# Loading k and q in pairs of blocks and transposing them in 64-column halves, in a fused attention and MLP kernel

## The chip, the core and the metric

The kernel runs on one core of one Trainium2 chip. The metric is device time in microseconds (us), the median of several runs. A core has TensorE (PE, with its weight loads shown as PEld), VectorE (DVE), ScalarE (ACT), GpSimd (POOL), SyncE (SP) and 16 DMA engines.

## What is computed

Sliding-window attention with a linear distance bias, then a two-layer MLP with a squared ReLU. Batch 8, 8 heads, 576 tokens, head size 64; the MLP goes from 512 to 2048 and back, over 4608 tokens.

```
scores = scale * q @ k.T ; bias = -slope[h] * |i - j|
mask   = (i - j >= 0) & (i - j < 128)
attn   = softmax(where(mask, scores + bias, -1e9))
x      = (attn @ v), heads side by side, as 4608 x 512
out    = square(relu(x @ w_in)) @ w_out
```

All inputs are float32 in device memory; the kernel works in bfloat16 and gives float32.

## The kernel before

Each batch entry is cut into five blocks of tokens: four of 128 and one of 64, 40 blocks in all. For each block m the function `attention` does these steps:

- q and k, loaded with tokens on partitions (a tile `kq`, 128 partitions, k in the first half of a row, q in the second), are turned so that the head dimension lies on partitions (`kqT`). For blocks 0 to 9 (`m < KQ_DMA`) TensorE does it: eight transposes of 128x128 into one PSUM bank (`tp`), evicted in two copies, one for k, one for q. For later blocks a DMA transpose from SyncE does it.
- One burst of score matmuls (`ps_s`, L361) with this block's and the previous block's keys. Each uses 64 rows of the array, and neighbouring ones use the two halves.
- ScalarE takes the exponential (L374), VectorE multiplies with a mask that holds bias and window (L382), TensorE multiplies with v (`pv`, L397; a column of ones in `vt` gives the sum of the row), VectorE normalises into `x` (L418, L423).
- x is transposed too (`xp`, L442, into `xT`), by TensorE for the first 13 blocks.

The MLP works on groups of 512 tokens. `fc_step` makes 128 hidden units for a group (`h`, L477), or, for the first two groups, several of them for a part of the group as its tokens become ready: group 0 in parts of 128 tokens, with four sets of hidden units for each step, so that one step needs one quarter of w_in. ScalarE applies the ReLU (L487) and VectorE or ScalarE squares (L495, L497). The second layer is plain for group 0 (`o`, L628), and for the other groups a scheme with seven products instead of eight (`o`, L559), with sums on VectorE (L523).

All loads are DMAs issued from GpSimd, which also convert to bfloat16 (k, q and v at L290, w_in at L256, w_out at L263). A load of a block has one piece of 64 floats for each token and head. `FIRST` (L162) is the order of the loads for the first ten blocks: `b3` means k, q and v of block 3, `i1` a quarter of w_in, `o1` a quarter of w_out.

The order of instructions on every engine is fixed before the launch. Each piece of work is a task with possible engines and estimated durations, a key (lower first), what it depends on and the buffers that it takes and frees. `Plan.order` runs through estimated time and picks, for each engine, the task that can start first, and among equals the one with the lowest key. The instructions are then emitted in that order; on the chip each engine works through its own list in order and waits where data are late.

Buffers are rings: a new user of a tag takes the slot of the oldest user, once all that read it are done. PSUM has "h" (2 banks: first-layer results, and for the first batch entry also `tp` and `xp`), "o" (2 banks: second-layer results, `pv` of the first five blocks, every second first-layer step of group 0) and "a" (4 banks: a burst of scores takes all four; `tp` and `xp` of later batch entries take one). In SBUF, `kq` has 4 slots, `vt` 6 and `kqT` 4.

Of the kernel before, what the change touches and what calls it, by code (L numbers as in the profile page):

```python
# [9 lines left out]
BF16 = mybir.dt.bfloat16  # L10
# [132 lines left out]
def kernel(  # L143
    ctx: ExitStack, tc: tile.TileContext, q, k, v, moe_w_in, moe_w_out, out
):
    nc = tc.nc

    B, H, S, D = q.shape
# [6 lines left out]
    NKB = (S + 127) // 128  # L155
    blk = [min(128, S - kb * 128) for kb in range(NKB)]
    C = d_model // 128
# [1 line left out]
    NG = NT // 512  # L159
    NBLK = B * NKB  # L160

    FIRST = "b0 i0 b1 i1 b2 i2 b3 i3 b4 b5 b6 o0 b7 o1 b8 o2 b9 o3"  # L162
    SPLIT = ([(0, 128), (128, 256), (256, 384), (384, 512)], [(0, 256), (256, 512)])

    KQ_DMA, X_DMA = 10, 13
# [3 lines left out]
    psum = ctx.enter_context(tc.tile_pool(name="psum", bufs=2, space=bass.MemoryType.PSUM))  # L169
    work = ctx.enter_context(tc.tile_pool(name="work", bufs=2))  # L170

    ident = const.tile([128, 128], BF16)
# [8 lines left out]
    def ring(name, n, shape):  # L181
        return [const.tile(shape, BF16, name=f"{name}_{i}") for i in range(n)]
# [4 lines left out]
    kq = ring("kq", size["kq"], [128, 2, d_model])  # L187
    vt = ring("vt", size["v"], [128, H, D + 1])
    kqT = ring("kqT", size["kqT"], [128, 2 * C, 128])
# [3 lines left out]
    plan = Plan({"h": 2, "o": 2, "a": 4, "rec": 4, "rt": 3, "g": 2, "S": 2, "osb": 4,  # L193
                 "s1": 2, "u2": 2, "x1": 2, **size})

    def act(n):
        return n * 0.84 + 90.0

    def dve(n, rate=1):
        return n / rate / 0.96 + 72.0  # L200

    def mm(n):
        return max(n, 64) / 2.4 + 1.5
# [12 lines left out]
    t_ident = plan.add({"DVE": 230.0}, -9e5 - 1, build_ident, [t_iota])  # L216
# [11 lines left out]
    def place(h):  # L228
        c, half = divmod(h, 2)
        return 4 * (c // 2) + 2 * half + c % 2  # L230
# [12 lines left out]
    t_ones = plan.add({"DVE": 1200.0}, -9e5 + 1, ones)  # L243


    def load(key, ns, emit, deps=(), acq=()):
        return plan.add({"POOL": 900.0}, key, emit, deps, acq, dma=ns)
# [29 lines left out]
    s_in, t_in = {}, {}  # L277

    def load_block(m, key):
# [4 lines left out]
        for i, (nm, src) in enumerate((("k", k), ("q", q), ("v", v))):  # L284
# [5 lines left out]
                nc.gpsimd.dma_start(o, src[b, :, kb * 128:kb * 128 + n, :].rearrange("h s d -> s h d"))  # L290
            t_in[m, nm] = load(key + 0.01 * i, 1050.0 * n / 128, emit, [t_ones] if nm == "v" else [], [sl])

    for i, what in enumerate(FIRST.split()):
        {"b": load_block, "i": load_w_in, "o": load_w_out}[what[0]](int(what[1:]), -9e5 + i)
    for m in range(2 * NKB, NBLK):
        load_block(m, -5e5 + m)

# [2 lines left out]
    chain = {"tp": [], "s": [], "pv": [], "xp": []}  # L300

    def copy(task, o, i):
        if task.eng == "DVE":
            nc.vector.tensor_copy(o, i)  # L304
        else:
            nc.scalar.activation(o, i, AF.Copy)  # L306

    def attention(m):
        b, kb = divmod(m, NKB)
        n = blk[kb]  # L310
        due = (b * S + kb * 128 + n) / 4 - 192 - 40
        first = b == 0
# [4 lines left out]
        sk = sk_of[m] = Slot("kqT")  # L317
        both = {"ACT": act(C * n), "DVE": dve(C * n, 2)}
        if kq_by_dma:
            def turn_kq():  # L320
                nc.sync.dma_start_transpose(kqT[sk.idx], kq[s_in[m, "k"].idx].rearrange("s t f -> s (t f)"))
            t_kq = [plan.add({"SP": 2000.0}, due - 80, turn_kq, [t_in[m, "k"], t_in[m, "q"]], [sk],
                             [s_in[m, "k"]], dma=1400.0)]
        else:
            slot = Slot("h" if first else "a")
            last = None
            for i in range(2 * C):
                def emit(i=i):
                    if i == 0:
                        slot.tile = psum.tile([128, 1024], BF16, tag=slot.tag, bufs=plan.bufs[slot.tag], name="tp")  # L330
                    nc.tensor.transpose(slot.tile[:, i * 128:(i + 1) * 128],  # L331
                                        kq[s_in[m, "k"].idx][:, i // C, (i % C) * 128:(i % C + 1) * 128], ident)
                last = plan.add({"PE": mm(128)}, due - 56, emit,
                                [last, t_ident, t_in[m, "kq"[i // C]]] + ([t_in[m, "q"]] + chain["tp"] if i == 0 else []),
                                [slot, sk] if i == 0 else [], [s_in[m, "k"]] if i == 2 * C - 1 else [])
            chain["tp"] = [last]
            t_kq = []
            for i in range(2):
                def evac(i=i):
                    copy(t_kq[i], kqT[sk.idx][:, i * C:(i + 1) * C, 0:n],  # L340
                         slot.tile[:, i * 512:(i + 1) * 512].rearrange("p (c s) -> p c s", c=C)[:, :, 0:n])
                t_kq.append(plan.add(both if first else {("DVE", "ACT")[i]: both[("DVE", "ACT")[i]]},
                                     due - 56, evac, [last], [], [slot]))
        t_kq_of[m] = t_kq


# [41 lines left out]
        for hf in range(2):  # L388
            slot_v = Slot("o" if m < 5 else "h")
            last = None  # L390
            for hi in range(4):
                h = 4 * hf + hi
                for part, mk in parts:
                    def emit(h=h, hi=hi, part=part, mk=mk, slot_v=slot_v):
                        if hi == 0 and part == p0:
                            slot_v.tile = psum.tile([128, 512], FP32, tag=slot_v.tag, bufs=plan.bufs[slot_v.tag], name="pv")
                        nc.tensor.matmul(  # L397
                            slot_v.tile[:, hi * (D + 1):(hi + 1) * (D + 1)],
                            Pt[sP.idx][:, place(h), part, :], vt[s_in[mk, "v"].idx][:, h, :],
                            start=part == p0, stop=part == 1)  # L400
                    rel = []
                    if hf == 1 and hi == 3:
                        if part == 0 or kb == NKB - 1:
                            rel.append(s_in[mk, "v"])
                        if part == 1:
                            rel.append(sP)
                    new = hi == 0 and part == p0
                    last = plan.add({"PE": mm(D + 1)}, due - 12 + 4 * hf, emit,
                                    [last, t_P[place(h) // 2], t_in[mk, "v"]]
                                    + (t_P[2 * hf:2 * hf + 2] + chain["pv"] if new else []),  # L410
                                    ([slot_v] + ([sx] if hf == 0 else [])) if new else [], rel)
# [18 lines left out]
        t0 = b * S + kb * 128  # L430
        if x_by_dma:
            def turn_x():
                nc.sync.dma_start_transpose(xT[:, :, t0:t0 + n], xt[sx.idx][0:n, :])
            t_xT[b, kb] = plan.add({"SP": 1280.0}, due, turn_x, t_norm, [], [sx], dma=1800.0)
        else:
            slot_x = Slot("h" if first else "a")
            last = None
            for c in range(C):
                def emit(c=c):
                    if c == 0:  # L440
                        slot_x.tile = psum.tile([128, 1024], BF16, tag=slot_x.tag, bufs=plan.bufs[slot_x.tag], name="xp")
                    nc.tensor.transpose(slot_x.tile[:, c * 128:(c + 1) * 128],  # L442
                                        xt[sx.idx][:, c * 128:(c + 1) * 128], ident)
                last = plan.add({"PE": mm(128)}, due, emit, [last] + t_norm,
                                [slot_x] if c == 0 else [], [sx] if c == C - 1 else [])

            def evac():
                copy(t_xT[b, kb], xT[:, :, t0:t0 + n],
                     slot_x.tile[:, 0:512].rearrange("p (c t) -> p c t", c=C)[:, :, 0:n])
            t_xT[b, kb] = plan.add(both if first else {"DVE": both["DVE"]}, due, evac, [last], [], [slot_x])  # L450

    sk_of, t_kq_of = {}, {}
    for m in range(NBLK):
        attention(m)

# [187 lines left out]
    key = 0  # L643
# [5 lines left out]
    for g in range(NG):  # L649
# [8 lines left out]
        key = base + (64 if g == 0 else 128)  # L658
# [36 lines left out]
```

## Time and profile before

| | |
|---|---|
| median of 3 runs | 307.44 us (307.18 to 307.74) |
| the profiled execution | 308.27 us |
| its span in the profile | 306.1 us |
| busy: PE, DVE, ACT, POOL | 289.8, 212.2, 200.0, 107.6 us |
| granted TensorE clock | 1.0 |
| moved by DMA | 39.31 MB, 128 GB/s on average |

The span is the time between the first and the last record of the program, about 2.2 us less than the execution's own time. In the rows of the profile, "L331" is line 331 of the kernel, `out<-in` names tiles of the program, "x80" counts instructions, and the time in brackets is how long the engine stood idle before the row and what released it. The ends of matmuls are modelled: one with 128 columns is shown with 0.22 us though the next one can start after 0.06, so start times are what is to be compared.

### The profile page before, as it was taken

To read this page: it belongs to the slowest core of one execution; us is meant where nothing else is said; L and a number is where in the kernel's file an instruction comes from. 1 tells how busy PE (TensorE), PEld (TensorE's weight loads), DVE (VectorE), ACT (ScalarE), POOL (GpSimd) and SP (SyncE) were. 2 spreads that over 40 slices of the span, in tenths; PEclk is the share of its full clock that TensorE was granted. 3 is DMA by queue.
4 is the path that set the end of the run, shared out by engine and by line. 5 is a ranking of instruction groups with operands and counts; after the bars stand their busy time and mean duration, and the time that the engine had idled before them with its cause. 6 is when DMAs were issued, how large, how long until landed. Compare 5 with 4: busy or idle time off the path is not lost.

```text
span 306.1 us, 7855 instructions
## 1 busy us (share of the span) xinstructions
PE 289.8 (95%) x3076; PEld 205.9 (67%) x3076; DVE 212.2 (69%) x633; ACT 200.0 (65%) x395; POOL 107.6 (35%) x133
## 2 busy tenths in 40 slices
PE   1489999999999999999999999999999999999995
PEld 1279987686866677666666666666766676666783
DVE  4348888749968786678758776677677785545622
ACT  4178894759769666767767787777667785564410
POOL 8747938626265444226361327132200000000000
PEclk9999999999999999999999999999999999999999
DMA  8999999999999999999999999999884112201223
GB/s 60 179 175 166 151 189 173 130 184 139 151 151 144 164 157 169 155 154 182 165 153 166 156 139 149 130 165 146 139 55 120 30 42 62 69 0 36 69 72 103
DMA packets 170901, 39.31 MB, mean 128 GB/s; under 512 B 158064, under 2 KB 170352, under 8 KB 170864
## 3 DMA queue, kind: packets, MB, share of 16 engines
q0 software_dynamic: 116736, 18.36, 93.9%
q1 hardware_dynamic: 54128, 20.46, 41.3%
q8 instruction: 24, 0.39, 0.5%
q14 instruction: 13, 0.11, 0.1%
HBM read 36.70 MB, written 9.44 MB: 151 GB/s over the span
## 4 chain that ended last, share of the span: by engine, by line
PE 92%; DMA 3%; DVE 2%; POOL 2%; ACT 1%; issue 0%; POOLq 0%; DVEq 0%
PE h L477 42%; PE o L559 32%; PE ps_s L361 6%; PE pv L397 6%; PE o L628 4%; DMA kq<-in_q_dram 3%; PE tp L331 1%; POOL kq L290 1%; PE xp L442 1%; ACT kqT L306 1%; DVE w_mix L273 0%; DVE kqT L304 0%; POOL vt L290 0%; DVE osb L593 0%; POOL w_in_sb L256 0%
## 5 line engine op out<-in xcount | busy, mean ns | idle before, releaser
L477 PE MATMUL h<-xT,w_in_sb 128*128 128x512 bf16 (+2 forms) x832 | 150.8, 316 | 0.3 <-DVE x L423 0.3
L487 ACT ACTIVATE rt<-h 128x512 bf16<-128x512 f32 x144 | 86.0, 600 | 61.9 <-PE h L477 54.2
L477 PEld LDWEIGHTS <-w_in_sb 128*128 128x128 bf16 x832 | 71.0, 99 | 35.4 <-DVE x L423 0.8
L374 ACT ACTIVATE P<-ps_s 128x512 bf16<-128x512 f32 (+1 forms) x160 | 71.1, 520 | 9.7 <-PE ps_s L361 9.5
L495 DVE TENSOR_TENSOR g<-rt 128x512 bf16<-128x512 bf16 x91 | 38.3, 422 | 35.1 <-ACT rt L487 34.4
L382 DVE TENSOR_TENSOR P<-P,masks 128x512 bf16<-128x512 bf16 (+1 forms) x160 | 54.4, 364 | 8.0 <-ACT P L374 6.5
L559 PEld LDWEIGHTS <-g 128*128 128x128 bf16 x512 | 47.9, 98 | 15.1
L290 POOL DMA_DIRECT2D kq<-in_k_dram x40 | 34.2, 855 | 55.6 <-DMA kqT<-kq 48.4
L290 POOL DMA_DIRECT2D vt<-in_v_dram x40 | 34.1, 856 | 52.8 <-PE pv L397 46.6
L559 PEld LDWEIGHTS <-S 128*128 128x128 bf16 x384 | 35.8, 98 | 11.7 <-issue 0.7
L559 PE MATMUL o<-w_mix,S 128*128 128x256 bf16 x256 | 38.7, 273 | 0.0
L559 PE MATMUL o<-w_mix,g 128*128 128x256 bf16 x256 | 37.5, 273 | 0.0
L559 PE MATMUL o<-w_out_sb,g 128*128 128x256 bf16 x256 | 36.9, 273 | 0.0
L290 POOL DMA_DIRECT2D kq<-in_q_dram x40 | 34.3, 857 | 2.0 <-DMA kq<-in_k_dram 1.3
L497 ACT ACTIVATE g<-rt 128x512 bf16<-128x512 bf16 x53 | 33.5, 632 | 1.3
L423 DVE TENSOR_TENSOR x<-pv,rec 128x256 bf16<-128x256 f32 (+1 forms) x80 | 33.3, 417 | 1.1
L397 PEld LDWEIGHTS <-P 128*128 128x128 bf16 x576 | 27.3, 98 | 8.9 <-DVE P L382 1.2
L397 PE MATMUL pv<-vt,P 128*128 128x65 bf16 x576 | 31.5, 194 | 0.6 <-DVE P L382 0.6
L418 DVE RECIPROCAL rec<-pv 128x4 f32<-128x4 f32 (+1 forms) x80 | 14.2, 177 | 14.6 <-PE pv L397 14.2
L361 PEld LDWEIGHTS <-kqT 64*128 64x128 bf16 x576 | 15.7, 96 | 11.1 <-issue 8.9
L361 PE MATMUL ps_s<-kqT 64*128 64x128 bf16 (+1 forms) x320 | 20.1, 216 | 0.8 <-DVE kqT L304 0.8
L361 PE MATMUL ps_s<-kqT,kqT 64*128 64x128 bf16 (+1 forms) x256 | 17.0, 214 | 1.4 <-ACT kqT L306 1.4
(41 smaller groups left out, 190.6 us busy)
## 6 DMA issues: line engine op xcount, KB each, us to landing
out_dram<-osb SPq DMA_DIRECT2D x35, 256.0 KB, 4.3
kq<-in_k_dram POOLq DMA_DIRECT2D x32, 128.0 KB, 7.1
kq<-in_q_dram POOLq DMA_DIRECT2D x32, 128.0 KB, 7.4
vt<-in_v_dram POOLq DMA_DIRECT2D x32, 128.0 KB, 8.2
w_in_sb<-in_moe_w_in_dram POOLq DMA_DIRECT2D x4, 512.0 KB, 9.8
w_out_sb<-in_moe_w_out_dram POOLq DMA_DIRECT2D x4, 512.0 KB, 10.0
kq<-in_k_dram POOLq DMA_DIRECT2D x8, 64.0 KB, 9.2
kq<-in_q_dram POOLq DMA_DIRECT2D x8, 64.0 KB, 8.9
```

Of the source, the lines that this page charges most:

```text
L290: nc.gpsimd.dma_start(o, src[b, :, kb * 128:kb * 128 + n, :].rearrange("h s d -> s h d"))
L361: nc.tensor.matmul(slot_s[2 * (c // 2) + half].tile.rearrange("p (c t q) -> p c t q", c=2, t=2)[:, c % 2, part, 0:n], kqT[sk_of[mk].idx][r ...
L374: nc.scalar.activation(view(Pt[sP.idx][:, 2 * i:2 * i + 2]), view(slot_s[i].tile.rearrange("p (c t q) -> p c t q", c=2, t=2)), AF.Exp, bia ...
L382: nc.vector.tensor_tensor(pt, pt, view(masks[:, 2 * i:2 * i + 2]), op=ALU.mult)
L397: nc.tensor.matmul(slot_v.tile[:, hi * (D + 1):(hi + 1) * (D + 1)], Pt[sP.idx][:, place(h), part, :], vt[s_in[mk, "v"].idx][:, h, :], star ...
L418: nc.vector.reciprocal(srec.tile[0:n, :], pv[0:n, :, D])
L423: nc.vector.tensor_tensor(xt[sx.idx][0:n, hf * 256:(hf + 1) * 256].rearrange("p (h e) -> p h e", h=4), pv[0:n, :, 0:D], srec.tile[0:n, :]. ...
L477: nc.tensor.matmul(slot.tile[:, f * w:(f + 1) * w], w_in_sb[:, cc, (fc + f) * 128:(fc + f + 1) * 128], xT[:, cc, g * 512 + lo:g * 512 + hi ...
L487: nc.scalar.activation(srt.tile, slot.tile, AF.Relu, bias=0.0, scale=1.0)
L495: nc.vector.tensor_tensor(o, i, i, op=ALU.mult)
L497: nc.scalar.activation(o, i, AF.Square)
L559: nc.tensor.matmul(bank.tile[:, t * 256:(t + 1) * 256], left(g, what, j)[:, t * 128:(t + 1) * 128], right(by, j), start=opens and j == 0 a ...
```

## The change

For blocks 0 to 9, k and q are no longer loaded block by block, but for a pair of neighbouring blocks: 256 tokens (64 for the fifth block of a batch entry, which stands alone). A tile `kq` holds one of k or q, and each partition has two neighbouring tokens: row p holds, for each head, the 64 values of token 2p and then the 64 of token 2p+1. A piece of a load is thus 128 floats. v is loaded block by block as before, and `FIRST` gets a new order, in which `s0` is k and q of the first pair and `v0` is v of block 0.

TensorE transposes such a tile in halves of 64 columns: one instruction takes one head of one of the two tokens of a partition (64 columns), and writes 64 partitions of PSUM and 128 columns. Even heads go to the lower 64 partitions, odd heads to the upper. k and q have a bank each. For a pair of blocks there are 16 halves for k and 16 for q.

The evictions are still two for each block, one for k and one for q. They read the bank with the two tokens of a pair 128 elements apart, so that `kqT` is written in the order of the tokens. For the second batch entry k is evicted by ScalarE and q by VectorE (before: k by VectorE, q by ScalarE).

```diff
-    FIRST = "b0 i0 b1 i1 b2 i2 b3 i3 b4 b5 b6 o0 b7 o1 b8 o2 b9 o3"
+    FIRST = "s0 i0 v0 v1 i1 s1 v2 i2 v3 i3 s2 v4 s3 v5 v6 o0 s4 v7 o1 v8 o2 s5 v9 o3"
...
+    def load_pair(i, key):
+        b, pr = divmod(i, (NKB + 1) // 2)
+        ms = [m for m in (b * NKB + 2 * pr, b * NKB + 2 * pr + 1) if m < (b + 1) * NKB]
+        n = sum(blk[m - b * NKB] for m in ms)
+        t0 = pr * 256
+        for j, (nm, src) in enumerate((("k", k), ("q", q))):
+            sl = Slot("kq")
+
+            def emit(src=src, sl=sl):
+                nc.gpsimd.dma_start(
+                    kq[sl.idx][0:n // 2].rearrange("p t f -> p (t f)").rearrange("p (h e) -> p h e", h=H),
+                    src[b, :, t0:t0 + n, :].rearrange("h (p u) d -> p h (u d)", u=2))
+            t = load(key + 0.01 * j, 1150.0 * n / 256, emit, [], [sl])
+            for m in ms:
+                s_in[m, nm], t_in[m, nm] = sl, t
...
-            slot = Slot("h" if first else "a")
-            last = None
-            for i in range(2 * C):
...
-                    nc.tensor.transpose(slot.tile[:, i * 128:(i + 1) * 128],
-                                        kq[s_in[m, "k"].idx][:, i // C, (i % C) * 128:(i % C + 1) * 128], ident)
-                last = plan.add({"PE": mm(128)}, due - 56, emit,
...
+            for j, nm in enumerate("kq"):
+                if kb % 2 == 0:
+                    turned[nm] = slot = Slot("h" if first else "a"), []
+                    last = None
+                    for i, g in [(i, g) for i in range(2 * C) for g in range(2)]:
...
+                            nc.tensor.transpose(
+                                slot.tile[g * 64:(g + 1) * 64, i * 128:(i + 1) * 128],
+                                kq[s_in[m, nm].idx].rearrange("p t f -> p (t f)").rearrange(
+                                    "p (c g u d) -> p c u g d", c=C, g=2, u=2)[:, i // 2, i % 2, g], ident)
+                        last = plan.add({"PE": mm(128) / 2}, due - 56, emit,
...
+                slot, (done_tp,) = turned[nm]
+
+                def evac(j=j, slot=slot):
+                    o = kqT[sk.idx][:, j * C:(j + 1) * C, 0:n].rearrange("p c (s u) -> p c s u", u=2)
+                    s0 = 64 * (kb % 2)
+                    copy(t_kq[j], o, slot.tile.rearrange("p (c u s) -> p c s u", c=C, u=2)[:, :, s0:s0 + n // 2])
+                t_kq.append(plan.add(both if first else {("ACT", "DVE")[j]: both[("ACT", "DVE")[j]]},
+                                     due - 56, evac, [done_tp], [sk] if j == 0 else [], [slot]))
```

More of the change, by code (lines that the diff above doesn't have):

```diff
@@ L291, in load_block, with load_v, emit @@
             t_in[m, nm] = load(key + 0.01 * i, 1050.0 * n / 128, emit, [t_ones] if nm == "v" else [], [sl])
+    def load_v(m, key):
+        b, kb = divmod(m, NKB)
+        n = blk[kb]
+        sl = s_in[m, "v"] = Slot("v")
+        def emit():
+            nc.gpsimd.dma_start(vt[sl.idx][0:n, :, 0:D], v[b, :, kb * 128:kb * 128 + n, :].rearrange("h s d -> s h d"))
+        t_in[m, "v"] = load(key, 1050.0 * n / 128, emit, [t_ones], [sl])
+    def load_pair(i, key):
[12 more added lines that the diff above has]
+                s_in[m, nm], t_in[m, nm] = sl, t
     for i, what in enumerate(FIRST.split()):
-        {"b": load_block, "i": load_w_in, "o": load_w_out}[what[0]](int(what[1:]), -9e5 + i)
+        {"s": load_pair, "v": load_v, "i": load_w_in, "o": load_w_out}[what[0]](int(what[1:]), -9e5 + i)
     for m in range(2 * NKB, NBLK):
@@ L324, in attention @@
         else:
-            slot = Slot("h" if first else "a")
-            last = None
-            for i in range(2 * C):
[L328 to L331, printed above, removed]
-                                        kq[s_in[m, "k"].idx][:, i // C, (i % C) * 128:(i % C + 1) * 128], ident)
-                last = plan.add({"PE": mm(128)}, due - 56, emit,
-                                [last, t_ident, t_in[m, "kq"[i // C]]] + ([t_in[m, "q"]] + chain["tp"] if i == 0 else []),
-                                [slot, sk] if i == 0 else [], [s_in[m, "k"]] if i == 2 * C - 1 else [])
@@ L336, in attention @@
-            chain["tp"] = [last]
-            t_kq = []
[L338 to L343, printed above, removed]
+            t_kq = []
@@ new lines, in attention, with emit @@
+            for j, nm in enumerate("kq"):
[3 more added lines that the diff above has]
+                    for i, g in [(i, g) for i in range(2 * C) for g in range(2)]:
+                        def emit(i=i, g=g, nm=nm, slot=slot[0]):
+                            if i == 0 and g == 0:
+                                slot.tile = psum.tile([128, 1024], BF16, tag=slot.tag, bufs=plan.bufs[slot.tag], name="tp")
+                            nc.tensor.transpose(
[3 more added lines that the diff above has]
+                        last = plan.add({"PE": mm(128) / 2}, due - 56, emit,
+                                        [last, t_ident, t_in[m, nm]] + (chain["tp"] if i == 0 else []),
+                                        [slot[0]] if i == 0 and g == 0 else [],
+                                        [s_in[m, nm]] if i == 2 * C - 1 and g == 1 else [])
+                    chain["tp"] = [last]
+                    slot[1].append(last)
+                slot, (done_tp,) = turned[nm]
[5 more added lines that the diff above has]
+                                     due - 56, evac, [done_tp], [sk] if j == 0 else [], [slot]))
@@ L450, in attention @@
             t_xT[b, kb] = plan.add(both if first else {"DVE": both["DVE"]}, due, evac, [last], [], [slot_x])
-    sk_of, t_kq_of = {}, {}
+    sk_of, t_kq_of, turned = {}, {}, {}
     for m in range(NBLK):
```

## The prediction

> **What bounds the kernel now.** I read four views of the profile, in this order: busy shares and slices on the page, the waits of TensorE from 17 us on, the timeline of the first 30 us, the transfers of those microseconds.
>
> ```profile
> PE 289.8 (95%) x3076; PEld 205.9 (67%) x3076; DVE 212.2 (69%) x633; ACT 200.0 (65%) x395; POOL 107.6 (35%) x133
> PE   1489999999999999999999999999999999999995
> DMA  8999999999999999999999999999884112201223
> ```
>
> ```profile
> PE ps_s L361 <- ACT kqT L306: 0.7, 1, 0.7
> PE o L559 <- DVE osb L593: 0.5, 1, 0.5
> PE h L477 <- DVE x L423: 0.3, 1, 0.3
> ```
>
> TensorE is busy in every slice but the first three and the last. The second fence is all that it waits for after 17 us: 1.5 us in 289. So the end is set by two things only: when dense work starts, and how much of it there is. The DMA engines are full in the first 30 of 40 slices, but after 17 us no TensorE wait names a load; transfers that finish earlier there are worth nothing by themselves.
>
> The start looks like this (start, length, engine, line, operation):
>
> ```profile
> 5.09 0.60 PE L331 MATMUL tp<-ident,kq 128*128 128x128 bf16 x4 [5.09 <-DMA kq<-in_k_dram]
> 6.35 0.61 PE L331 MATMUL tp<-ident,kq 128*128 128x128 bf16 x4 [0.65 <-DMA kq<-in_q_dram]
> 8.97 1.18 PE L397 MATMUL pv<-vt,P 128*128 128x65 bf16 x8 [0.56 <-DVE P L382]
> 10.42 0.42 DVE L423 TENSOR_TENSOR x<-pv,rec 128x256 bf16<-128x256 f32 x1
> 13.38 0.61 PE L331 MATMUL tp<-ident,kq 128*128 128x128 bf16 x4 [3.23 <-DMA kq<-in_k_dram]
> 14.21 0.61 PE L331 MATMUL tp<-ident,kq 128*128 128x128 bf16 x4 [0.22 <-DMA kq<-in_q_dram]
> 14.62 0.63 PE L442 MATMUL xp<-ident,x 128*128 128x128 bf16 x4
> 15.29 0.42 DVE L304 COPY xT<-xp 128x512 bf16<-128x512 bf16 x1
> 16.93 3.24 PE L477 MATMUL h<-xT,w_in_sb 128*128 128x128 bf16 x32
> ```
>
> Block 0 is normalised at 10.84, but its transpose (14.62) stands behind block 1's k and q in TensorE's order, and those land only at 13.4 and 14.2. The first layer starts at 16.93.
>
> **The earlier start: a gain.** The change loads k and q of blocks 0 and 1 first, then the first quarter of w_in, then v of block 0. I need three paces of the DMA engines. The next rows are the issues of q, v and w_in, each one's time to landing (in the same order), and packets in 4 to 6 us, 18 to 20 us and 26 to 28 us.
>
> ```profile
> 2.26 0.89 POOL L290 DMA_DIRECT2D kq<-in_q_dram  x1
> 3.53 1.02 POOL L290 DMA_DIRECT2D vt<-in_v_dram  x1
> 4.55 0.76 POOL L256 DMA_DIRECT2D w_in_sb<-in_moe_w_in_dram  x1
> kq<-in_q_dram POOLq DMA_DIRECT2D x1, 128.0 KB, 4.0
> vt<-in_v_dram POOLq DMA_DIRECT2D x1, 128.0 KB, 4.7
> w_in_sb<-in_moe_w_in_dram POOLq DMA_DIRECT2D x1, 512.0 KB, 7.9
> DMA packets 1437, 0.18 MB, mean 90 GB/s; under 512 B 1437, under 2 KB 1437, under 8 KB 1437
> DMA packets 576, 0.41 MB, mean 203 GB/s; under 512 B 204, under 2 KB 576, under 8 KB 576
> DMA packets 2348, 0.31 MB, mean 156 GB/s; under 512 B 2328, under 2 KB 2348, under 8 KB 2348
> ```
>
> A 128-token load is 1024 packets of 128 bytes. With the engines full (last row, 2328 in 2 us) it takes 0.88 us, or 2 x 16 / 2328 = 13.7 ns of an engine per packet. In 18 to 20 us, 204 such packets use 2.8 of 32 engine-us, so 372 packets of 1 KB take 29.2 / 372 = 78 ns each, and a w_in quarter of 512 of them 2.5 us. A pair load is 1024 packets of 256 bytes, a size that the trace does not have. On a straight line between the two it is 22.9 ns, so 1.47 us for what two loads do in 1.76; at worst it costs twice a small packet (1.76), at best its bytes at 1 KB price, 19.5 ns (1.25). At the very start the packets come slower (1437 in 2 us, 1024 in 1.43 us), GpSimd writing one load per 0.9 to 1.0 us. There a pair load takes about as long as a single one does now: the pair of k and q lands near 5.2 and 6.4 instead of 5.1 and 6.3.
>
> Then comes w_in. In the rows it landed at 12.45 (4.55 + 7.9), 4.2 us after v (8.23). I take those 4.2 again: 10.6. v of block 0 adds 0.88: 11.5. From v to the first layer it needs 1.87 for the products with v and their normalising (8.97 to 10.84), and about 1.2 for the transpose of x and its eviction (0.63 + 0.42 and hand-overs): 3.1, so the first layer starts at 14.6 instead of 16.93. I enter **-2.2**. Bounds: 1.4 if a packet of 256 bytes costs two small ones (0.3 for each of the two pair loads) and the lag lasts a little longer; 3.0 if w_in lands in 3.4 us instead of 4.2 (by its pace alone it takes 2.5). I go no further, because TensorE must still find work at every moment after that start, with pair 1 landing two pair loads after the second w_in quarter.
>
> **More TensorE work: a loss.** In steady state, the transposes and the tiled score matmuls run like this:
>
> ```profile
> 34.04 0.41 PE L397 MATMUL pv<-vt,P 128*128 128x65 bf16 x8
> 34.28 0.39 PE L477 MATMUL h<-xT,w_in_sb 128*128 128x128 bf16 x4
> 36.69 0.61 PE L331 MATMUL tp<-ident,kq 128*128 128x128 bf16 x8
> 37.13 1.22 PE L477 MATMUL h<-xT,w_in_sb 128*128 128x128 bf16 x19
> 38.42 0.29 PE L397 MATMUL pv<-vt,P 128*128 128x65 bf16 x4
> 38.64 0.23 PE L361 MATMUL ps_s<-kqT,kqT 64*128 64x128 bf16 x2
> 39.04 0.22 PE L361 MATMUL ps_s<-kqT 64*128 64x128 bf16 x2
> 39.19 0.30 PE L397 MATMUL pv<-vt,P 128*128 128x65 bf16 x4
> ```
>
> Eight transposes go from 36.69 to 37.13: 55 ns each. Sixteen score matmuls, which use 64 rows of the array each, run two at a time: 14 of them from 38.64 to 39.04, 28.6 ns each. But they start 0.10 us after the four products ahead of them are issued (4 x 30 ns from 38.42, by 8 in 0.24 at 34.04), and the next product comes at 39.19, 0.09 after they end at 39.10. A change of the array's tiling and back costs 0.19 us.
>
> The change has 16 half transposes per tensor and pair: 192 for six pairs, in place of 80. Pair 0's fall into waiting time at the start, so 160 stand against 64 of blocks 2 to 9 (64 x 55 ns = 3.5 us). No row shows a half over 64 columns. Its price lies between 28 ns (two at a time, as the score matmuls) and 56 (one after the other, each still streams 128 columns of the identity). I take 28, since the halves alternate between column groups as the scores do between row groups: 4.5 us, **+0.9**. By 56 it is 9.0, +5.4.
>
> Against 28 speaks the Trainium skill, "TensorEngine Tiling (Array Packing)", Restrictions: column tiling switches the fast weight load off. Its page "TensorE: Matmul & The Clock Gate", LDWEIGHTS, gives columns / 1.2 ns, an estimate of 53 ns for 64 columns. In this trace 128 columns load in 30 ns or less (the eight products at 34.04); no row has a load of 64 columns. If loads of the two column groups can't overlap, the sum goes to its upper end; rival A has that.
>
> Each run of halves also switches the tiling, as today's full transposes do not. k and q of a pair land about 1.4 us apart, so pairs 1, 3 and 4 have two runs each, the two 64-token pairs one: 8 runs x 0.19 = **+1.5** (5 to 10 runs: 1.0 to 1.9).
>
> **Evictions and slots.**
>
> ```profile
> L304 DVE COPY kqT<-tp 128x512 bf16<-128x512 bf16 x9 | 3.7, 422 | 8.0 <-PE tp L331 5.7 <-PE pv L397 1.8 <-ACT kqT L306 0.4
> L306 ACT ACTIVATE kqT<-tp 128x512 bf16<-128x512 bf16 x7 | 4.2, 597 | 8.2 <-DVE kqT L304 7.9 <-PE tp L331 0.2
> L607 DVE TENSOR_TENSOR u<-o,s 128x512 f32<-128x512 f32 x1 | 0.7, 692 | 0.2 <-PE o L559 0.2
> ...
> 45.00:50.00 5.00, 5.00 (x45) 3.14 (x44) 5.00 (x18) 2.39 (x5) 3.41 (x4) 1.00 1.85 180
> ```
>
> There are 20 evictions as before. They now read PSUM with neighbouring elements 128 apart. ScalarE should stay at 597; VectorE lies between 422 and the 692 of an operation that takes one element at a time, so up to 0.27 more, some 3 us over ten copies. The Trainium skill, "VectorE: DVE Perf Modes", asks for steps of one in its doubled mode, which speaks for 692; the copies with steps of one take 422 here, and no row has another step. TensorE's queue of other work hides this, but VectorE is full in 45 to 50 us (5.00 of 5.00), and TensorE once waited on it (0.3): **+0.2** (0 to 0.8). k and q now lie in two banks, so both engines can evict at once; the 0.7 us wait of ps_s behind ACT kqT may go. On the other side, a pair holds both "h" slots until four evictions are done, and two of four "a" slots later, while first-layer steps and the transpose of x want "h". One eviction time of 0.6 to 0.7 for two waiting steps is 1.3; it falls in the densest stretch for pair 1 alone. Together **+0.3** (-0.7 to +1.3). Fewer GpSimd issues (12 for 20) end nothing that is late.
>
> **Sum:** -2.2 + 0.9 + 1.5 + 0.2 + 0.3 = +0.7. The profiled execution took 308.27 (span 306.1 and 2.2 around it), 0.83 over the median of 307.44. The difference of 0.7 in the span is added to the median: **308.1**.
>
> **Rivals.** A: the halves do not run two at a time, or are not tiled by columns at all. +5.4 for +0.9 gives +5.2, 312.6; without tiling the 1.5 of switches go too, 311.1. Nothing in the trace shows column groups side by side; the row groups speak against it. It decides from about 36 ns a half, where it alone adds 1.3.
> B, faster: the loads win more. w_in lands 3.4 us after q, the start is 3.0 earlier, k and q of a pair are transposed in one run (5 runs, 1.0), and the ps_s wait of 0.7 goes without a new one: -3.0 + 0.9 + 1.0 - 0.7 + 0.2 = -1.6, 305.8. For it: the 4.2 us of the first w_in quarter is long against 2.5. Against: TensorE's order is fixed, so any load that is late stops it. It decides where the start gains over 2.9.
> C: packets of 256 bytes cost no less per byte than small ones, and TensorE, in order, waits for pair 1: the gain falls to 0.8, the sum to +2.1, 309.5.
>
> **The numbers.** The forecast has 0.48, A 0.21, B 0.23, C 0.08. A change under 0.2% (0.6 us) can't be told from none, the runs lying from 307.18 to 307.74. The forecast's own range is 306.8 to 309.4; of its 0.48, 0.05 is faster, 0.20 the same and 0.23 slower. So faster 0.28, same 0.20, slower 0.52. The range reaches from 305.9, near B, to 312.6, A.
>
> **What would show it.** The first h matmul near 14.6; pair loads of about 1.5 us; 192 tp matmuls, 32 within about 0.9 us and 0.1 us gaps on both sides; VectorE's kqT copies at 692; TensorE's waits after 17 us still under 3 us. I am wrong if h starts after 16, if 16 halves take 0.9 us, or if new waits on kqT or on loads stand in the dense part.

## The result, and the profile after

The changed kernel took 310.56 us (median of four runs) against 307.31 us: the ratio is 1.0094, with a 95% interval of 1.0068 to 1.0121. One of the four, the profiled one, ran at a granted clock of 0.573 and took 506.76 us; the ratio leaves it out (the median of the other three is 310.41). Run again, as e1 below, the changed kernel took 310.28 us against 308.34 us, 1.0072 (1.0050 to 1.0094). By these two ratios it is slower by 2.2 to 2.9 us where +0.7 was forecast; both medians lie in the stated range of 305.9 to 312.6, but above the likeliest case's own range, which ended at 309.4. The profile shown here is that of e1: span 308.6 us, 2.5 more than before.

The page, busy time by engine, then TensorE's slices and its granted clock:

```profile
PE 293.8 (95%) x3188; PEld 207.5 (67%) x3188; DVE 215.0 (70%) x627; ACT 202.7 (66%) x401; POOL 100.1 (32%) x125
...
PE   2589999999999999999999999999999999999995
...
PEclk9999999999999999999999999999999999999999
```

TensorE is again the engine that is never idle after the start, and it has 112 matmuls more. All its waits that the view names, start included:

```profile
PE tp L359 <- DMA kq<-in_k_dram: 7.1, 2, 5.8
PE pv L430 <- DMA vt<-in_v_dram: 2.0, 1, 2.0
PE ps_s L394 <- DVE kqT L329: 0.8, 1, 0.8
PE xp L475 <- DVE x L456: 0.7, 2, 0.5
PE o L592 <- DVE osb L626: 0.5, 1, 0.5
PE tp L359 <- DMA kq<-in_q_dram: 0.3, 1, 0.3
```

TensorE's timeline of the start (start, length, what; the wait in brackets):

```profile
5.83 1.06 PE L359 MATMUL tp<-ident,kq 128*64 128x128 bf16 x16 [5.83 <-DMA kq<-in_k_dram]
7.19 1.06 PE L359 MATMUL tp<-ident,kq 128*64 128x128 bf16 x16 [0.30 <-DMA kq<-in_q_dram]
...
11.62 0.38 PE L430 MATMUL pv<-vt,P 128*128 128x65 bf16 x4 [1.97 <-DMA vt<-in_v_dram]
...
14.03 0.40 PE L475 MATMUL xp<-ident,x 128*128 128x128 bf16 x2 [0.52 <-DVE x L456]
14.36 0.69 PE L430 MATMUL pv<-vt,P 128*128 128x65 bf16 x5
16.29 1.07 PE L359 MATMUL tp<-ident,kq 128*64 128x128 bf16 x16 [1.24 <-DMA kq<-in_k_dram]
17.29 0.35 PE L430 MATMUL pv<-vt,P 128*128 128x65 bf16 x3
17.44 0.30 PE L510 MATMUL h<-xT,w_in_sb 128*128 128x128 bf16 x1
17.53 0.65 PE L430 MATMUL pv<-vt,P 128*128 128x65 bf16 x8
17.99 1.57 PE L510 MATMUL h<-xT,w_in_sb 128*128 128x128 bf16 x13
19.50 1.06 PE L359 MATMUL tp<-ident,kq 128*64 128x128 bf16 x16
20.49 1.82 PE L510 MATMUL h<-xT,w_in_sb 128*128 128x128 bf16 x18
```

v of block 0 lands at 11.6, as forecast, and x of block 0 is transposed by 14.4. But TensorE's fixed order then wants the transposes of pair 1, whose k lands only at 16.3, and the first layer starts at 17.4, half a microsecond later than before (16.93). By then TensorE has, however, done eight of block 1's products with v and the transposes of pair 1's k, which the kernel before does only after 16.93. The same timeline in the dense part:

```profile
25.80 3.01 PE L510 MATMUL h<-xT,w_in_sb 128*128 128x128 bf16 x51
28.73 0.64 PE L359 MATMUL tp<-ident,kq 128*64 128x128 bf16 x16
29.30 0.66 PE L430 MATMUL pv<-vt,P 128*128 128x65 bf16 x16
29.89 0.64 PE L359 MATMUL tp<-ident,kq 128*64 128x128 bf16 x16
```

A run of 16 halves takes 0.57 us from its first start to the next product: 16 x 28 ns, 0.02 more for its first pair, and 0.10 for the change back. The change into the tiling costs 0.09 ahead of 28.73, so a run pays 0.22 for its tiling.

**The ledger.** To see where 2.5 us come from, take the starts of all matmuls in a trace and set each gap to the next one against the pace of the same matmul in a dense stretch: 0.056 us for 128 columns, 0.216 for 512, and in a tiled run 0.056 for a pair (0.003 to the second of the pair, 0.053 to the next pair). A surplus at a change of tiling, or in the first pair behind it, is booked there. A surplus over 0.3 us before 25 us, or over 0.15 at a change of tiling and 0.04 elsewhere after it, is a wait. What is left before 25 us is mostly matmuls at the slow pace: in the first 20 us those of 128 columns start about 0.11 us apart. The last line is the start of the last matmul. Differences from the kernel before, in us, one profiled run each:

| | e1, changed | e2, whole slices | e3, late pair 1 | e4, halves alone | e5, first entry | e6, first entry, late |
|---|---|---|---|---|---|---|
| first matmul later by | 0.73 | 0.75 | 0.76 | -0.35 | 0.71 | 0.68 |
| transposes at their pace | 0.90 | 0.90 | 0.90 | 0.00 | 0.45 | 0.45 |
| changes of tiling (more of them) | 2.33 (18) | 0.30 (0) | 1.75 (18) | 2.22 (20) | 1.36 (8) | 0.54 (3) |
| waits before 25 us | -2.55 | -3.14 | -2.33 | 0.01 | -2.57 | -1.20 |
| slow matmuls before 25 us | 0.65 | 0.65 | 0.02 | -0.83 | 0.55 | -0.37 |
| waits 25 to 60 us | 0.39 | 1.68 | 0.47 | -0.27 | 0.57 | 1.57 |
| waits after 60 us | 0.00 | 0.24 | 1.47 | 0.00 | 0.14 | 0.00 |
| rest | 0.08 | 0.07 | 0.11 | 0.05 | 0.03 | 0.05 |
| last matmul | 2.52 | 1.44 | 3.15 | 0.83 | 1.24 | 1.71 |

### The profile page after: what moved, and what is told of

Same layout as the page of the kernel before. It is cut to its first block, busy times and chain, and to the rows that moved or that the text cites. A ratio compares the mean times of both kernels' runs of the same rounds, so it can differ in the third digit from the quotient of the medians.

```text
span 505.0 us, 8026 instructions
## 1 busy us (share of the span) xinstructions
PE 484.5 (96%) x3151; PEld 280.4 (56%) x3188; DVE 218.2 (43%) x627; ACT 207.3 (41%) x401; POOL 100.2 (20%) x125
## 4 chain that ended last, share of the span: by engine, by line
PE 95%; DMA 2%; issue 2%; POOL 1%; DVE 0%; POOLq 0%; DVEq 0%
PE h L510 43%; PE o L592 34%; PE pv L430 6%; PE ps_s L394 5%; PE o L661 5%; DMA kq<-in_k_dram 2%; PE tp L359 2%; PE xp L475 1%; POOL kq L311 0%; POOL w_in_sb L256 0%; POOL vt L299 0%; DVE osb L626 0%; POOL dist L208 0%; POOLq L208 0%; DVEq L626 0%
## 5 line engine op out<-in xcount | busy, mean ns | idle before, releaser
L510 PE MATMUL h<-xT,w_in_sb 128*128 128x512 bf16 (+2 forms) x803 | 243.3, 456 | 5.1 <-issue 2.9
L510 PEld LDWEIGHTS <-w_in_sb 128*128 128x128 bf16 x832 | 96.7, 130 | 80.7 <-issue 59.5
L592 PEld LDWEIGHTS <-g 128*128 128x128 bf16 x512 | 63.5, 128 | 46.1 <-issue 23.8
L592 PE MATMUL o<-w_mix,S 128*128 128x256 bf16 x256 | 62.0, 387 | 0.0
L592 PE MATMUL o<-w_mix,g 128*128 128x256 bf16 x256 | 60.3, 385 | 0.0
L592 PE MATMUL o<-w_out_sb,g 128*128 128x256 bf16 x256 | 59.5, 382 | 0.2 <-issue 0.2
L430 PEld LDWEIGHTS <-P 128*128 128x128 bf16 x576 | 39.1, 119 | 21.7 <-issue 15.5
L430 PE MATMUL pv<-vt,P 128*128 128x65 bf16 x576 | 43.8, 232 | 1.4 <-DMA vt<-in_v_dram 1.2
L592 PE MATMUL o<-w_out_sb,S 128*128 128x256 bf16 x128 | 28.7, 385 | 0.5 <-DVE osb L626 0.5
L394 PEld LDWEIGHTS <-kqT 64*128 64x128 bf16 x576 | 19.7, 110 | 16.9 <-issue 15.0
L661 PE MATMUL o<-w_out_sb,g 128*128 128x512 bf16 x56 | 25.6, 576 | 1.2 <-issue 0.5
```

The lines of the kernel that those rows point to most:

```text
L394: nc.tensor.matmul(slot_s[2 * (c // 2) + half].tile.rearrange("p (c t q) -> p c t q", c=2, t=2)[:, c % 2, part, 0:n], kqT[sk_of[mk].idx][r ...
L430: nc.tensor.matmul(slot_v.tile[:, hi * (D + 1):(hi + 1) * (D + 1)], Pt[sP.idx][:, place(h), part, :], vt[s_in[mk, "v"].idx][:, h, :], star ...
L510: nc.tensor.matmul(slot.tile[:, f * w:(f + 1) * w], w_in_sb[:, cc, (fc + f) * 128:(fc + f + 1) * 128], xT[:, cc, g * 512 + lo:g * 512 + hi ...
L592: nc.tensor.matmul(bank.tile[:, t * 256:(t + 1) * 256], left(g, what, j)[:, t * 128:(t + 1) * 128], right(by, j), start=opens and j == 0 a ...
L661: nc.tensor.matmul(bank.tile, g_slots[g].tile[:, fc, t * 128:(t + 1) * 128], w_out_sb[:, fc], start=fc == 0, stop=fc == FCB - 1)
```

## The experiments

Each kernel was timed in turn with the kernel before on the same chip. The executions of one kernel differ by about 1 us either way, so a ledger of one run and the interval of the ratios have to be read together. In the code, `...` stands for lines left out.

**e1, the changed kernel**, without an edit.

> The changed kernel itself, for a profile at the full clock. Theory S (the start): its products start as early as forecast, but the first h matmul stands behind the transposes of pair 1, so it starts at 16.8 to 17.4 us, no earlier than before (16.9); TensorE's work grows by 2 to 3 us; total 310.0 to 310.8. Rival H (the halves run one after the other, 56 ns each): h starts near 14.6 and a run of 16 halves takes 0.9 us when warm. Rival W (new waits): TensorE waits 2 us or more on kqT or on PSUM slots after 17 us.

Measured: 310.28 us, ratio 1.0072 (1.0050 to 1.0094). The rows above decide: h starts at 17.4 (theory S), a run of halves takes 0.57 us and not 0.9 (against H), and the waits after 17 us in the view are 0.7 us (against W as it was stated; the ledger has 0.4 us more waiting than before at 25 to 60 us, in pieces under 0.4 us that the view mostly doesn't list).

**e2, whole slices.** The right arrangement of k and q is left out.

```diff
-                    for i, g in [(i, g) for i in range(2 * C) for g in range(2)]:
+                    for i in range(2 * C):
...
-                                slot.tile[g * 64:(g + 1) * 64, i * 128:(i + 1) * 128],
+                                slot.tile[:, i * 128:(i + 1) * 128],
-                                kq[s_in[m, nm].idx].rearrange("p t f -> p (t f)").rearrange(
-                                    "p (c g u d) -> p c u g d", c=C, g=2, u=2)[:, i // 2, i % 2, g], ident)
+                                kq[s_in[m, nm].idx].rearrange("p t f -> p (t f)")[:, i * 128:(i + 1) * 128], ident)
...
```

> Eight whole transposes of 128 neighbouring columns for each pair and tensor in place of sixteen halves; the heads then lie in the wrong places, so what is left out is the right arrangement of k and q. Loads and evictions as changed. Theory S: 160 x 28 ns less 80 x 55 ns is about nothing for the halves, and 8 to 10 changes of tiling of 0.19 us go: 1.5 to 2 us less than the changed kernel. Rival H: 4.5 us less for the halves and 1.5 for the tiling, 6 us less. Rival W: within 0.6 us of the changed kernel.

Measured: 310.48 us, ratio 1.0072 (1.0047 to 1.0097): no gain that the runs can tell, as rival W had it, though the trace has 2.0 us less for changes of tiling and its last matmul is 1.1 us earlier than e1's. (The profiled run, 309.36 us, was the fastest of the six.) The waits of TensorE in its trace after 17 us:

```profile
PE o L591 <- DVE osb L625: 0.5, 1, 0.5
PE tp L359 <- DMA kq<-in_k_dram: 0.5, 1, 0.5
PE xp L474 <- DVE x L455: 0.4, 1, 0.4
PE tp L359 <- DMA kq<-in_q_dram: 0.2, 1, 0.2
```

Part of what is taken out comes back as waits for k and q of later pairs and for x (1.7 us at 25 to 60 us against 0.4). Theory S's 1.5 to 2 us were not measured; the two intervals leave room for about 1 us. So this run doesn't show that the kernel gets back what the changes of tiling cost; that they are a cost is shown by e4.

**e3, pair 1 later.** One more dependency, so that its transposes come behind the first 32 h matmuls:

```diff
...
+    plan.tasks[first_tp[2, "k"]].deps.append(h_last[0, 4, 0])
     done = plan.order()
```

> The changed kernel, with the transposes of pair 1 placed behind the first 32 h matmuls in TensorE's order (one more dependency in the plan). Theory S: h starts at 14.6 to 15.2, about 2 us less than the changed kernel, 308 to 308.8. Rival W: the later kqT of pair 1 makes new waits, no gain or slower. Rival H: no gain, since the start was not what was lost.

Measured: 311.14 us, ratio 1.0102 (1.0067 to 1.0137). Theory S failed; no gain or slower was rival W's forecast. TensorE's timeline in e3, and its wait behind DMA transposes:

```profile
15.79 0.37 PE L511 MATMUL h<-xT,w_in_sb 128*128 128x128 bf16 x2
15.95 0.65 PE L431 MATMUL pv<-vt,P 128*128 128x65 bf16 x8
16.41 2.39 PE L511 MATMUL h<-xT,w_in_sb 128*128 128x128 bf16 x23
...
26.09 1.29 PE L360 MATMUL tp<-ident,kq 128*64 128x128 bf16 x32 [0.92 <-DMA kq<-in_k_dram]
...
PE ps_s L395 <- DMA kqT<-kq: 0.9, 2, 0.5
```

The first layer does start 1.6 us earlier (15.8 for 17.4). At 26.1 TensorE stands before pair 2, whose k has just landed, and later before DMA transposes of later blocks (ps_s behind kqT, the larger part of 1.5 us after 60 us). The time won was given back, to loads that land later and not to the later `kqT` of pair 1.

**e4, the halves alone**, in the kernel before:

```diff
-            for i in range(2 * C):
+            for i, g in [(i, g) for i in range(2 * C) for g in range(2)]:
...
-                    nc.tensor.transpose(slot.tile[:, i * 128:(i + 1) * 128],
-                                        kq[s_in[m, "k"].idx][:, i // C, (i % C) * 128:(i % C + 1) * 128], ident)
+                    c0 = (i % C) * 128 + g * 64
+                    nc.tensor.transpose(slot.tile[g * 64:(g + 1) * 64, i * 128:(i + 1) * 128],
+                                        kq[s_in[m, "k"].idx][:, i // C, c0:c0 + 64], ident)
...
```

> The kernel before, with each 128-column transpose cut into two halves of 64 columns; loads and evictions as before. Theory S: 128 halves of 28 ns for 64 whole ones of 55 is nothing, 8 runs with two changes of tiling are 1.5 us: 308.5 to 309.2. Rival H: 128 x 56 less 64 x 55 is 3.6 us, with the tiling 5.1: 312.4. Rival W: 307.3 to 307.8, since evictions and slots are those of before.

Measured: 309.63 us, ratio 1.0063 (1.0038 to 1.0088), 1.2 to 2.7 us slower. S gave 1.2 to 1.9 over the kernel before, H 5.1, W none: S holds. By the ratios the halves alone cost nearly as much as the whole change (1.0063 and 1.0072, within the intervals), so what the pair loads win at the start is about what they cost elsewhere. TensorE's timeline in e4:

```profile
36.58 0.64 PE L332 MATMUL tp<-ident,kq 128*64 128x128 bf16 x16
37.15 1.24 PE L478 MATMUL h<-xT,w_in_sb 128*128 128x128 bf16 x19
```

Sixteen halves of a block take 0.57 us to the next matmul, where the same block's eight whole transposes took 0.44. The halves are as cheap as the whole ones; the changes of tiling around them, 20 more, are 2.2 us in the ledger. (This profiled run began 0.35 us earlier, lost 0.8 less at the slow pace and waited 0.3 less, and was the fastest of the seven; that is why its last matmul is only 0.8 later.)

**e5, pairs in the first batch entry only.** Blocks 5 to 9 are loaded and transposed as before.

```diff
-    FIRST = "s0 i0 v0 v1 i1 s1 v2 i2 v3 i3 s2 v4 s3 v5 v6 o0 s4 v7 o1 v8 o2 s5 v9 o3"
+    FIRST = "s0 i0 v0 v1 i1 s1 v2 i2 v3 i3 s2 v4 b5 b6 o0 b7 o1 b8 o2 b9 o3"
...
```

> Pairs only for the first batch entry (blocks 0 to 4); blocks 5 to 9 are loaded, transposed and evicted as before. Theory S2 (TensorE pays for each change of tiling, 0.22 us a run, for the halves, and for small waits at 42 to 49 us, while the start gains only 0.7): the three later pairs with five runs go, so 1.1 for the tiling, 0.5 for halves and up to 1 for waits less: 0.3 to 0.8 us over the kernel before. Rival D (the start alone is what costs; the later pairs are free): no change from the changed kernel, 2 to 2.5 us over the kernel before.

Measured: 309.05 us against 307.96, ratio 1.0024 (1.0005 to 1.0043), 0.7 us over the kernel before, as S2 said; D is out. By the ratios of e1 and e5 the three later pairs cost about 1.5 us, and nothing shows that they bring any: no TensorE wait after 17 us named a load in the kernel before.

**e6, first entry only, and pair 1 late, k and q of a pair in one run.** The edits of e5 and e3, and

```diff
...
-                                        [last, t_ident, t_in[m, nm]] + (chain["tp"] if i == 0 else []),
+                                        [last, t_ident, t_in[m, nm], t_in[m, "q"]] + (chain["tp"] if i == 0 else []),
```

> As e5, and in addition k and q of a pair are transposed in one run, and those of pair 1 stand behind the first 32 h matmuls. Theory S2: h starts about 2 us earlier than in the changed kernel, as in e3, and with fewer later pairs no load has to be waited for after it; 1.0 to 1.5 us less than e5: 0.5 to 1 us faster than the kernel before. Rival L (the loads set the pace, so that time won at the start is lost at pair 2, as e3 lost it): within 0.5 us of e5.

Measured: 309.61 us, ratio 1.0056 (1.0036 to 1.0076), 0.6 to 1 us slower than e5. Theory S2 (0.5 to 1 us faster) failed; L had the direction, but its 0.5 us either way was too small. TensorE's waits in e6 after 17 us:

```profile
PE h L531 <- DMA w_in_sb<-in_moe_w_in_dram: 1.2, 1, 1.2
PE xp L496 <- DVE x L477: 1.2, 1, 1.2
PE h L531 <- ACT P L428: 0.9, 1, 0.9
PE o L614 <- DVE osb L648: 0.5, 1, 0.5
PE h L531 <- DVE x L477: 0.4, 1, 0.4
```

With fewer changes of tiling and an earlier h, TensorE now waits for a quarter of w_in (at 25.5), for x, and 0.9 us behind ScalarE.

**e7, evictions of neighbouring elements.** The order of the tokens inside a pair is left out.

```diff
-                    o = kqT[sk.idx][:, j * C:(j + 1) * C, 0:n].rearrange("p c (s u) -> p c s u", u=2)
-                    s0 = 64 * (kb % 2)
-                    copy(t_kq[j], o, slot.tile.rearrange("p (c u s) -> p c s u", c=C, u=2)[:, :, s0:s0 + n // 2])
+                    s0 = n * (kb % 2)
+                    copy(t_kq[j], kqT[sk.idx][:, j * C:(j + 1) * C, 0:n],
+                         slot.tile.rearrange("p (c s) -> p c s", c=C)[:, :, s0:s0 + n])
```

> The changed kernel with evictions that read neighbouring elements; what is left out is the order of the tokens inside a pair, so its output is another one. VectorE's copies go back from 687 to about 424 ns. Theory S2: VectorE is full for a few us at 40 to 44 only, so 0 to 0.5 us less than the changed kernel. Rival V (the strided copies delay the whole second batch entry): 1 us or more less.

Measured: 310.21 us, ratio 1.0071 (1.0045 to 1.0096), the same as the changed kernel: S2's 0 to 0.5 us fits, V's 1 us or more does not. The copies in e1's trace (count, then shortest/median/longest in ns):

```profile
L329 DVE COPY kqT<-tp x12: 415/687/692, 6.9 to 49.0; 128x512 bf16<-128x512 bf16 x10, 128x256 bf16<-128x256 bf16 x2
L331 ACT ACTIVATE kqT<-tp x8: 384/597/702, 18.1 to 48.5; 128x512 bf16<-128x512 bf16 x6, 128x256 bf16<-128x256 bf16 x2
```

and in e7's:

```profile
L329 DVE COPY kqT<-tp x12: 281/420/426, 6.8 to 48.8; 128x512 bf16<-128x512 bf16 x10, 128x256 bf16<-128x256 bf16 x2
L331 ACT ACTIVATE kqT<-tp x8: 383/597/688, 17.7 to 48.3; 128x512 bf16<-128x512 bf16 x6, 128x256 bf16<-128x256 bf16 x2
```

VectorE's copies go from 687 to 420 ns and the time doesn't move: TensorE's other work hid them.

**e8 and e9, the kernel before with a better order at the start.** Its loads and whole transposes stay; e8 places block 1's transposes behind the first 16 h matmuls, e9 only behind the transpose of x of block 0.

```diff
...
+    plan.tasks[first_tp[1]].deps.append(h_last[0, 0, 0])        # e8
+    plan.tasks[first_tp[1]].deps.append(t_xT[0, 0].deps[0])     # e9
     done = plan.order()
```

> The kernel before, with the transposes of block 1 placed behind the transpose of x of block 0 and the first 16 h matmuls (one more dependency in the plan); loads as before. In the kernel before x of block 0 is ready at 10.84, the first w_in quarter at 12.45, and h starts at 16.93 only because block 1's transposes stand ahead. Theory S2: most of what a better start can give lies in TensorE's order and not in the loads: h starts near 12.6, 1 us or more faster than the kernel before. Rival L (the loads set the pace, time won at the start is lost at the next load): waits for w_in or k and q appear after it and the time stays within 0.6 us, or gets worse.

> The kernel before, with only the transpose of x of block 0 placed ahead of the transposes of block 1. Theory S2: h starts 0.5 to 1 us earlier (the 0.6 of x's transpose and its eviction leave the way), 0.3 to 1 us faster. Rival L: within 0.6 us of the kernel before.

Measured: e8 309.25 us, ratio 1.0061 (1.0033 to 1.0089); e9 309.60 us, 1.0062 (1.0035 to 1.0089). Both slower; S2's part about the order fell. TensorE's timeline in e8:

```profile
11.97 1.89 PE L478 MATMUL h<-xT,w_in_sb 128*128 128x128 bf16 x16 [0.67 <-DMA w_in_sb<-in_moe_w_in_dram]
13.65 1.06 PE L332 MATMUL tp<-ident,kq 128*128 128x128 bf16 x8
17.06 1.07 PE L478 MATMUL h<-xT,w_in_sb 128*128 128x128 bf16 x16 [2.35 <-DMA w_in_sb<-in_moe_w_in_dram]
```

h starts five microseconds earlier, and after 16 of its matmuls the second quarter of w_in stops TensorE for 2.35 us. Booked as in the ledger, e8's waits before 25 us are 0.2 us longer than in the kernel before, and 0.9 us more goes to matmuls at the slow pace. In e9 h starts at 13.3 and TensorE is still 0.5 to 1 us ahead when as much has been done as the kernel before has done at 70 us; it loses that, and more, in two waits, 2.4 us together, for DMA transposes of k and q of later blocks:

```profile
PE ps_s L362 <- DMA kqT<-kq: 2.4, 2, 1.6
```

Moving one step at the start moves the whole plan behind it.

No kernel here beats the kernel before.

## Why the prediction was right and where its sum was off

The direction was right, and so was the frame: an earlier start against more TensorE work, with the second the larger. The start was not. "I am wrong if h starts after 16" was one of the prediction's own signs, and h starts at 17.4; both large terms, the start and the changes of tiling, were missed to the same side, by 1.0 and 0.8 us. That the total still lies in the stated range is owed to its width, which reaches up to rival A (16 halves in 0.9 us); A is out. Term by term, forecast and then e1's ledger:

- **Loads.** A pair load's packet was put at 22.9 ns on a straight line; from 14 to 16 us, nearly all packets being of that size, 1412 in 2 us are 2 x 16 / 1412 = 22.7 ns (e1's view of the DMA in that stretch):

```profile
DMA packets 1412, 0.36 MB, mean 182 GB/s; under 512 B 1404, under 2 KB 1412, under 8 KB 1412
```

  v of block 0 was forecast for 11.5 and its products start at 11.62. The first k and q were 0.6 and 0.8 us later than forecast (5.83, 7.19): at the start, too, the engines need some 1.5 us for a pair load (2 x 1024 / 1384), once the first packets have come. The same view for 4 to 6 us:

```profile
DMA packets 1384, 0.35 MB, mean 175 GB/s; under 512 B 1384, under 2 KB 1384, under 8 KB 1384
```

- **The start, -2.2.** This is the step that failed first. (16.93 less 14.6 is 2.3; the sum entered 2.2.) The sum went from v straight to h in 3.1 us, and the chain is there (11.62 to the transpose of x at 14.4). But between x and h stand the products of block 1 and a wait of 1.24 us for pair 1, with 1.0 for its transposes. The prediction had this in rival C (TensorE, in order, waits for pair 1), without the dear packets. The ledger has 2.55 less of waiting, of which 0.73 is lost by the later first matmul and 0.65 to matmuls at the slow pace, which here lasts until 21.9 us and in the kernel before until 19.7: **-1.2** in place of -2.2. Nor did the four tries at the order win more: e3, e6, e8 and e9 moved h forward and lost it to later loads and other waits.
- **Halves, +0.9:** +0.90 (the prediction's own 160 x 28 ns less 64 x 55 ns is 0.96). They run two at a time, 28 ns each. Rival A is out. The Trainium skill's rule for a weight load without the fast mode ("TensorE: Matmul & The Clock Gate", LDWEIGHTS, an estimate of 53 ns for 64 columns) gave 28 only if the loads of the two column groups overlap; with the measured 28 ns they don't stand in the way.
- **Changes of tiling, +1.5:** +2.33, under-sized by 0.8. The price in dense stretches was nearly right (0.22 us a run for 0.19), and so were nine runs for eight. After 25 us, 13 more changes are 1.4 us. The other 0.9 falls before 25 us: 0.6 on the changes around pair 1's two runs, which cost 0.19 each at the slow pace of TensorE (0.11 later), and 0.3 on changes around scores, some of which lie inside a wait or after 25 us in the kernel before.
- **Evictions, +0.2:** none by e7, though 687 ns came as forecast. **Slots and other waits, +0.3:** +0.39 at 25 to 60 us. That the size fits is not a proof of the cause: e1 has 1.0 us of pieces at 41.9 to 47.4 us, and a wait of 0.5 that the kernel before has at 56.6 us is gone. e7 keeps them, so it is not the strided copies, and e5 has 0.57 without the later pairs; e4's -0.27 shows how far single runs differ. VectorE and ScalarE are both full at that place, more than before (busy time by stretch, e1 and then the kernel before):

```profile
40.00:44.00 4.00, 3.73 (x66) 3.27 (x63) 4.00 (x16) 4.00 (x9) 0.88 (x1) 1.00 1.99 175
40.00:44.00 4.00, 4.00 (x77) 3.54 (x74) 3.94 (x13) 3.58 (x8) 1.80 (x3) 1.00 1.35 201
```

  (stretch, its length, then PE, PEld, DVE, ACT, POOL busy). Whether the order of loads, that of VectorE's work or the PSUM slots are to blame was not tried.

So the sum is -1.2 + 0.9 + 2.3 + 0.4 + 0.1 = 2.5 in place of 0.7: 1.0 us of the miss is at the start, 0.8 in the tiling. Rival B would have needed both the start and the single runs; e6 shows the second without profit.

## What to carry over

Work on an engine with a fixed order gains from an earlier load only if nothing that lands later stands ahead of the work to be started: follow the engine's list from the landing to the wanted instruction, and then to the next load behind it. A cheaper form of a matmul that needs another tiling of the array is to be priced with its changes, one for each run and side, and those early in the kernel at the slow pace. Where an engine is busy to the end, as here, parts of a change that only relieve other queues (the later pairs: 1.5 us) cost and bring nothing that the runs show.

## What the runs showed of the hardware

- Half transposes into the two column halves of the array run two at a time, as score matmuls in two row halves do: 28 ns each, against 55 for a whole one. Entering this tiling costs 0.09 us, its first pair 0.02 and leaving it 0.10 (e1, from 28.7 us on).
- A transfer's packets of 128, 256 and 1024 bytes take 13.7, 22.7 and 78 ns of an engine when all engines are full (the first and last worked out in the prediction, the second from e1).
- VectorE's PSUM copy of 512 two-byte elements takes 687 ns with a step of 128 and 420 with a step of one; ScalarE's takes 597 with either (e1 and e7).
- In the first 20 us matmuls of 128 columns start 0.105 to 0.107 us apart (13 of them from 17.99 in e1, before the change at 19.50) and later 0.056, though the page shows a granted clock of 1.0 in both. The Trainium skill, "TensorE: Matmul & The Clock Gate", Part 1, describes half speed until the engine has been busy for some 3.4 us. The two paces agree with it, but the clock row doesn't show them, and the slow pace ended 3.7 us after unbroken work began in the kernel before (15.97 to 19.7) and 5.6 us after it in e1 (16.3 to 21.9).
